# Attention step of a retention + mixture-of-experts kernel: the next step's scores moved behind the values, and the values' matmuls grouped by row half

## The chip, the cores and the metric

The program runs on one core of one Trainium2 chip. The time is the device time of one execution in microseconds. The kernel before takes 430.98 us (median of three timed runs, 430.73 to 432.25).

## The reference

Queries, keys and values are float32 of shape batch 8, heads 8, sequence 576, head dimension 64. Each head has a decay gamma; there is no softmax, so the attention is a masked and decayed product:

```python
scores = scale * np.matmul(q, k.transpose(0, 1, 3, 2))
Dmat = np.where(rel >= 0, gamma[:, None, None] ** rel[None, :, :], 0.0)
ret = scores * Dmat[None, :, :, :]
attn_out = np.matmul(ret, v)
```

The result, seen as 4608 tokens of 512 numbers (`x`), goes through one routed expert layer. A token with `x @ w_skip <= 0` is passed on unchanged. Each other token goes to the expert with the largest `x @ w_gate` (8 experts, hidden width 1024), and its output is `x + gate * (relu(x @ w1[e]) @ w2[e])`.

## The kernel before

**Two phases.** The first (some 157 us) is the attention and, beside it, the routing of the tokens; the second runs the experts. The change is in the first.

**Tiles of the attention.** The 4608 tokens are 36 tiles of 128 rows (`NT`), numbered `g`. Two batches are 9 tiles (`NPD`), so `place(g) = g % 9` is a tile's place; at place 0 a sequence begins, and at place 4 one ends in the first 64 rows and the next begins. The decays are powers of gamma, so a causal product over the whole sequence is taken as a product inside the tile plus a running 64x64 state per head:

- `load_u(g)` loads the tile: queries and keys by head (first half of `u`), values and keys by row (second half). Five tiles fit (`UBUFS`); tile `g + 4` is loaded into the buffer that tile `g - 1` leaves.
- `scale(g)` (L478): GpSimd multiplies the values by gamma to the minus position, in `u` itself.
- `scores(g)` (L446): eight matmuls, contraction 64, 128 columns, on the upper and lower half of the array's rows in turn (`r` = 0, 1). Half `r` fills the PSUM tile `psc[r]`, one bank each.
- `causal(g)` (L461): VectorE multiplies the two PSUM tiles by the mask and writes `sc` to SBUF, first `r` = 0, then `r` = 1.
- `state(g)` (L483): eight matmuls of 128 rows, 64 columns, which add the tile's keys times values to `ps_s`; ScalarE copies that to `st` for the next tile. None at place 8.
- `values(g)` (L503): eight matmuls (128 rows, 64 columns) of the scores with the values (L513), then eight with the state of the tiles before (64 rows, 64 columns, L527; none at place 0), all added up in two PSUM tiles `pxt` (names `xt0`, `xt1`). VectorE multiplies these by the decays into `xt` (L540).
- `stage_c(g)` (L547): four transposes, a copy by ScalarE and the store of the tile to `out`.

**Order.** TensorE's instructions stand in the order in which the code is written (a manual schedule for this engine). The other engines' orders are set by a scheduler, which places the routing's many small VectorE operations between `causal` and `xt`; each engine then runs its list strictly in order. One iteration `g` of the loop (L663 to L687) writes: `load_u(g + 4)`, `scale(g + 1)`, `scores(g + 1)`, `causal(g + 1)`, some filler matmuls in the first two iterations (`keep_up`), `state(g)`, `values(g)`, `stage_c(g - 1)`, and then routing matmuls. So the scores of a tile are made one iteration ahead of its values.

**Routing.** Every fourth iteration `logits_a` (L556) multiplies four tiles of `xt` by the gate weights, and an iteration later `logits_b` (L571) transposes the result (`pn`). After each group of 8, 8, 8, 4, 4, 4 tiles, `route_a` and `route_b` pick the expert, count, and rank the tokens in some 35 VectorE operations of 8 to 64 numbers a partition (L148 to L205), and `slot_match` (L212) makes one one-hot matrix a tile, which TensorE multiplies (L217). Near the end `close_first` (L266) gives the row numbers `gi` (L279) for the first gather of tokens from `out` (L287, GpSimd), behind which GpSimd splits the first experts' weights (L613).

Of the kernel before, what the change touches and what calls it, by code (L numbers as in the profile page):

```python
# [26 lines left out]
NPR = H // 2  # L27
# [30 lines left out]
def kernel(  # L58
# [25 lines left out]
    def keep_up(n):  # L84
        for _ in range(n):
            nc.tensor.matmul(ps_m, warm[:, :P], warm, start=True, stop=True)
# [312 lines left out]
    with ExitStack() as actx:  # L399
# [13 lines left out]
        def load_u(g):  # L413
            u_t[g] = ap.tile([P, 4, DM], F32, tag="u", name=f"u_{g}", bufs=UBUFS)
            for s in range(2):
                nc.sync.dma_start(u_t[g][:, 2 * s : 2 * s + 2].rearrange("p s i -> p (s i)"), qkv[g, s])
# [23 lines left out]
        def head(a, r):  # L440
            return 2 * a + (r ^ (a & 1))

        def place(g):
            return g % NPD

        def scores(g):  # L446

            u = u_t[g].rearrange("p s (a i) -> p s a i", a=NPR)
            psc_t[g] = [pp.tile([P, NPR, P], F32, tag=f"sc{r}", name=f"psc{r}_{g}") for r in range(2)]
            for a in range(NPR):  # L450
                for r in range(2):
                    nc.tensor.matmul(  # L452
                        psc_t[g][r][:, a, :],
                        u[halves[r], 1, a, :],
                        u[halves[r], 0, a, :],
                        start=a == 0,
                        stop=a == NPR - 1,
                        skip_group_check=True,
                    )

        def causal(g):  # L461

            sc_t[g] = ap.tile([P, 2, NPR, P], F32, tag="sc", name=f"sc_{g}")
            m = masks[place(g) == NPD // 2].unsqueeze(1).broadcast_to([P, NPR, P])
            for r, ps in enumerate(psc_t.pop(g)):
                nc.vector.tensor_tensor(sc_t[g][:, r], ps, m, ALU.mult)  # L466

        def decays(g):
            c0 = 2 * g % NQ
            ins = nc.vector.tensor_tensor(  # L470
                gt_sb[:, c0 : c0 + 2],
                gt_sb[:, 0:2],
                qt_sb[:, c0 : c0 + 2, :].unsqueeze(3).broadcast_to([P, 2, NPR, D]),
                ALU.mult,
            )
            tc.keep_in_program_order(ins)

        def scale(g):  # L478

            v = u_t[g][:, 2].rearrange("p (h i) -> p h i", h=H)  # L480
            nc.gpsimd.tensor_tensor(v, v, vt_sb[:, place(g), :].unsqueeze(2).broadcast_to([P, H, D]), ALU.mult)  # L481

        def state(g):  # L483

            t = place(g)
            if t == NPD - 1:
                return
            rows = slice(D, P) if t == NPD // 2 else slice(0, P)
            v, k = (u_t[g][rows, 2 + s].rearrange("p (h i) -> p h i", h=H) for s in range(2))
            for a in range(NPR):  # L490
                for r in range(2):
                    nc.tensor.matmul(
                        ps_s[halves[r], a, :],
                        k[:, head(a, r), :],
                        v[:, head(a, r), :],
                        start=t in (0, NPD // 2) and a == 0,
                        stop=a == NPR - 1,
                        skip_group_check=True,
                    )
            st_t[g + 1] = ap.tile([P, NPR, D], F32, tag="st", name=f"st_{g + 1}")  # L500
            nc.scalar.copy(st_t[g + 1], ps_s)

        def values(g):  # L503

            u = u_t[g].rearrange("p s (a i) -> p s a i", a=NPR)
            v = u_t[g][:, 2].rearrange("p (h i) -> p h i", h=H)
            pxt = px_t[g] = [pp.tile([P, NPR // 2, P], F32, tag=f"xt{e}", name=f"pxt{e}_{g}") for e in range(2)]
            sc = sc_t.pop(g)
            t = place(g)
            for a in range(NPR):  # L510
                for r in range(2):
                    j = head(a, r) % 2
                    nc.tensor.matmul(  # L513
                        pxt[a % 2][halves[j], a // 2, :],
                        v[:, head(a, r), :],
                        sc[:, r, a, :],
                        start=a < 2,
                        stop=t == 0 and a >= NPR - 2,
                        skip_group_check=True,
                    )  # L520
            if t:
                n = D if t == NPD // 2 else P
                st = st_t.pop(g)
                for a in range(NPR):
                    for r in range(2):
                        j = head(a, r) % 2
                        nc.tensor.matmul(  # L527
                            pxt[a % 2][halves[j], a // 2, :n],
                            st[halves[r], a, :],
                            u[halves[r], 0, a, :n],  # L530
                            start=False,
                            stop=a >= NPR - 2,
                            skip_group_check=True,
                        )
            b, o = divmod(g, NB)
            if o == 0:
                xt_t[b] = ap.tile([P, NPR, NB * P], F32, tag="xt", name=f"xt_{b}")
            c0 = 2 * g % NQ
            for e in range(2):
                nc.vector.tensor_tensor(  # L540
                    xt_t[b][:, e::2, o * P : (o + 1) * P].rearrange("p a (c i) -> p a c i", c=2),
                    pxt[e].rearrange("p a (c i) -> p a c i", c=2),
                    gt_sb[:, c0 : c0 + 2, e::2].rearrange("p c a i -> p a c i"),
                    ALU.mult,
                )

        def stage_c(g):  # L547
            b, o = divmod(g, NB)
            px = pp.tile([P, DM], F32, tag="xn", name=f"px_{g}")
            for c in range(NCC):  # L550
                nc.tensor.transpose(px[:, c * P : (c + 1) * P], xt_t[b][:, c, o * P : (o + 1) * P], ident)  # L551
            xn = ap.tile([P, DM], F32, tag="xn", name=f"xn_{g}")
            nc.scalar.copy(xn, px)  # L553
            nc.scalar.dma_start(out[g * P : (g + 1) * P, :], xn)
# [16 lines left out]
        def logits_b(b, lt):  # L571
            pn = pp.tile([P, NB, P], F32, tag="lg", name=f"pn_{b}")
            for o in range(NB):
                nc.tensor.transpose(pn[:, o, :], lt[:, o * P : (o + 1) * P], ident)
            nc.vector.tensor_reduce(
                lg[:, b * NB : (b + 1) * NB, :],
                pn.rearrange("p t (c w) -> p t w c", w=WP)[:, :, :NW, :],
                axis=AX.X,
                op=ALU.add,
            )  # L580
# [45 lines left out]
        def routing(most):  # L626

            for do in added:
                do()
            added.clear()  # L630
            for n in range(most):
                if not todo or len(added) == NR or todo[0][1] > g or (n and todo[0][0]):
                    break
                todo.pop(0)[2]()
# [28 lines left out]
        for g in range(NT):  # L663
            ahead = g + 1 < NT
            if g + UAHEAD < NT:
                load_u(g + UAHEAD)
            if ahead:
                scale(g + 1)
                scores(g + 1)
                causal(g + 1)  # L670
            if g < len(NKEEP):
                keep_up(NKEEP[g])
            state(g)
            values(g)
            if g < 4:
                decays(g + 1)
            if g:
                stage_c(g - 1)
            if lt is None:
                routing(1 if g == NT - 1 else 3 if g < starts[KCUT + 1] else 8)  # L680
            if lt is not None:
                logits_b(g // NB - 1 - (g % NB < 2), lt)
                route(g // NB - 1 - (g % NB < 2))
                lt = None
            if g > NB and g % NB == 1:
                lt = logits_a(g // NB - 1)
            weights()  # L687
        g = NT
# [328 lines left out]
```

## Time and profile before

| | us |
|---|---|
| median of the timed runs | 430.98 |
| the profiled execution's own time | 431.52 |
| its span, first to last instruction | 429.8 |
| attention phase, first scores to the last values' transposes | 5.7 to 157.3 |
| TensorE busy over the span | 408.5 (95%) |
| VectorE busy over the span | 270.5 (63%) |
| granted TensorE clock, mean | 0.982 |

The span is 1.7 us shorter than the time of the same execution; what lies around it is launch and end. TensorE's busy time is a union of modelled matmul times, so it says that work was in flight, and not that the array ran at its peak. A float32 matmul of the program shows as two records, so eight matmuls are "x16"; only a transpose is one record. Weight loads are shown as an engine of their own (PEld).

### The profile page before, as it was taken

The page shows a single profiled execution, that of the slowest core. Times are in us where ns is not written, and L with a number is a line of the kernel's source. Part 1 is how long each engine was busy: PE and PEld are TensorE (multiplying, and loading weights), DVE is VectorE, ACT ScalarE, POOL GpSimd, SP SyncE. Part 2 cuts the span into 40 slices and gives each one's busy share as a digit, 9 for nine tenths or more (in the row PEclk, how much of TensorE's full clock was granted, in tenths as well). Part 3 has the DMA queues.
Part 4 walks back from the last instruction along what each step waited for, and adds up shares of the span by engine and source line. Part 5 has one row for each costly group of instructions (what it writes and reads, how often), then busy time and mean ns, then how long its engine had stood idle before and what let it go on. Part 6 is the DMA issues. An engine that isn't in the chain of part 4 may idle for free. (4 is left out here: it accounts for less than half of the span.)

```text
span 429.8 us, 10717 instructions
## 1 busy us (share of the span) xinstructions
PE 408.5 (95%) x4303; PEld 363.1 (84%) x4303; DVE 270.5 (63%) x636; ACT 152.6 (36%) x264; POOL 115.1 (27%) x133
## 2 busy tenths in 40 slices
PE   7999999999999968999999999999999999999990
PEld 3878778777787855888999999999999999999990
DVE  3665596596488989738655654875655655656421
ACT  1222322222223443117434434434444445445210
POOL 4332232122123475150330042032141230400402
PEclk9999999999999996999999999999999999999995
DMA  8999998998899764355663445455465465642101
GB/s 316 397 363 322 356 317 282 316 318 278 304 325 355 310 192 152 101 149 202 202 227 128 146 168 197 148 165 194 148 203 165 158 203 188 208 132 95 51 2 52
DMA packets 28869, 91.71 MB, mean 213 GB/s; under 512 B 4104, under 2 KB 4232, under 8 KB 28817
## 3 DMA queue, kind: packets, MB, share of 16 engines
q1 hardware_dynamic: 19584, 71.31, 49.2%
q0 software_dynamic: 3616, 9.86, 6.8%
q10 hardware_dynamic: 5616, 9.82, 6.0%
q8 instruction: 35, 0.57, 0.5%
q14 instruction: 18, 0.14, 0.1%
HBM read 76.80 MB, written 14.55 MB: 213 GB/s over the span
## 5 line engine op out<-in xcount | busy, mean ns | idle before, releaser
L137 DVE TENSOR_TENSOR wlo_w<-w,whi_w 128x1024 fp32r<-128x1024 f32 x59 | 71.9, 1223 | 62.3 <-ACT whi_w L136 62.3
L136 ACT CAST whi_w<-w 128x1024 fp32r<-128x1024 f32 x59 | 61.7, 1051 | 61.3 <-PE py L371 59.8
L800 POOL DMA_INDIRECT out<-rs,sidx x24 | 32.8, 1367 | 158.3 <-DVE rs L799 155.0
L371 PE MATMUL py<-hhi,whi_w 128*128 128x344 f32 (+6 forms) x224 | 70.7, 316 | 0.0
L371 PE MATMUL ph<-xhi,whi_w 128*128 128x344 f32 (+6 forms) x224 | 68.9, 307 | 0.0
L371 PE MATMUL ph<-xhi,wlo_w 128*128 128x344 f32 (+6 forms) x224 | 67.8, 302 | 0.0
L371 PE MATMUL ph<-xlo,whi_w 128*128 128x344 f32 (+6 forms) x224 | 67.7, 302 | 0.0
L371 PE MATMUL py<-hlo,whi_w 128*128 128x344 f32 (+6 forms) x224 | 67.6, 302 | 0.0
L371 PE MATMUL py<-hhi,wlo_w 128*128 128x344 f32 (+6 forms) x224 | 67.6, 302 | 0.0
L481 POOL TENSOR_TENSOR u<-u,tt_sb 128x512 f32<-128x512 f32 x36 | 38.3, 1063 | 104.6 <-DMA u<-qkv 88.3
L466 DVE TENSOR_TENSOR sc<-psc,mask 128x512 f32<-128x512 f32 x72 | 46.6, 684 | 25.6 <-PE psc L452 25.6
L379 ACT ACTIVATE hhi<-ph 128x344 fp32r<-128x344 f32 (+8 forms) x61 | 26.0, 427 | 64.6 <-PE ph L371 59.0
L452 PEld LDWEIGHTS psc<-u 64*128 64x128 f32 x576 | 36.7, 187 | 13.6 <-DVE xt L540 5.4
L452 PE MATMUL psc<-u 64*128 64x128 f32 x576 | 44.3, 285 | 2.2 <-DMA u<-qkv 1.3
L553 ACT COPY xn<-px 128x512 f32<-128x512 f32 x36 | 21.1, 586 | 64.4 <-PE px L551 44.1
L371 PEld LDWEIGHTS py<-hhi,whi_w 128*128 128x128 f32 x224 | 42.2, 188 | 0.9
L371 PEld LDWEIGHTS ph<-xhi,whi_w 128*128 128x128 f32 x224 | 42.2, 188 | 0.2
L371 PEld LDWEIGHTS ph<-xlo,whi_w 128*128 128x128 f32 x224 | 42.2, 188 | 0.1
L371 PEld LDWEIGHTS py<-hlo,whi_w 128*128 128x128 f32 x224 | 42.2, 189 | 0.0
L371 PEld LDWEIGHTS ph<-xhi,wlo_w 128*128 128x128 f32 x224 | 42.2, 189 | 0.0
L371 PEld LDWEIGHTS py<-hhi,wlo_w 128*128 128x128 f32 x224 | 42.2, 188 | 0.0
L380 DVE SCALAR_TENSOR_TENSOR hlo<-ph,hhi 128x344 fp32r<-128x344 f32 (+8 forms) x61 | 28.9, 474 | 15.8 <-ACT hhi L379 14.8
(179 smaller groups left out, 616.6 us busy)
## 6 DMA issues: line engine op xcount, KB each, us to landing
u<-qkv SPq DMA_DIRECT2D x72, 512.0 KB, 6.6
w<-w SPq DMA_DIRECT2D x64, 512.0 KB, 3.6
out<-xn ACTq DMA_DIRECT2D x36, 256.0 KB, 6.7
out<-rs,sidx POOLq DMA_INDIRECT x24, 4.8
xg<-out,gidx POOLq DMA_INDIRECT x21, 5.1
gt_sb<-gtab ACTq DMA_DIRECT2D x1, 256.0 KB, 5.7
wg_sb<-wg ACTq DMA_DIRECT2D x1, 64.0 KB, 6.7
tt_sb<-ttab ACTq DMA_DIRECT2D x1, 56.0 KB
```

What stands on the lines that cost most here:

```text
L136: nc.scalar.copy(hi, t)
L137: nc.vector.tensor_tensor(lo, t, hi.bitcast(F32), ALU.subtract)
L371: nc.tensor.matmul(ps, x, y, start=first and n == 0, stop=last and n == 3 * len(terms) - 1)
L379: nc.scalar.activation(hi, ph, AF.Relu)
L380: nc.vector.scalar_tensor_tensor(lo, ph, 0.0, hi.bitcast(F32), ALU.max, ALU.subtract)
L452: nc.tensor.matmul(psc_t[g][r][:, a, :], u[halves[r], 1, a, :], u[halves[r], 0, a, :], start=a == 0, stop=a == NPR - 1, skip_group_check=True,
L466: nc.vector.tensor_tensor(sc_t[g][:, r], ps, m, ALU.mult)
L481: nc.gpsimd.tensor_tensor(v, v, vt_sb[:, place(g), :].unsqueeze(2).broadcast_to([P, H, D]), ALU.mult)
L553: nc.scalar.copy(xn, px)
L800: put = nc.gpsimd.indirect_dma_start(out=out, out_offset=bass.IndirectOffsetOnAxis(ap=sidx[:n, k, e : e + 1], axis=0), in_=rs[:n], in_offs ...
```

## The change

Two edits. In `values`, the loop over the row half `r` is now outside the loop over the pairs `a`: the four matmuls that read `sc[:, 0]` come first, then the four that read `sc[:, 1]`. In the iteration, `state(g)` and `values(g)` now come before `scores(g + 1)` and `causal(g + 1)`.

```diff
@@ -507,8 +507,8 @@
             pxt = px_t[g] = [pp.tile([P, NPR // 2, P], F32, tag=f"xt{e}", name=f"pxt{e}_{g}") for e in range(2)]
             sc = sc_t.pop(g)
             t = place(g)
-            for a in range(NPR):
-                for r in range(2):
+            for r in range(2):
+                for a in range(NPR):
                     j = head(a, r) % 2
                     nc.tensor.matmul(
                         pxt[a % 2][halves[j], a // 2, :],
@@ -666,12 +666,13 @@
                 load_u(g + UAHEAD)
             if ahead:
                 scale(g + 1)
+            state(g)
+            values(g)
+            if ahead:
                 scores(g + 1)
                 causal(g + 1)
             if g < len(NKEEP):
                 keep_up(NKEEP[g])
-            state(g)
-            values(g)
             if g < 4:
                 decays(g + 1)
             if g:
```

TensorE in iteration 11, before (the names are those of the text above; a number behind a name is the buffer's, the bracket names the semaphores waited for, by the engine that raises them; rows that read like the one above them but for the buffer are left out):

```order
L452 MATMUL psc_12_823<-u_634 128x128 [waits DMAHW1_49,DVE_49]
L452 MATMUL psc_12_824<-u_634 128x128 [waits DVE_49]
L492 MATMUL ps_s<-u_579 64x64 [waits DMAHW0_49,Activation_49,Pool_49]
L492 MATMUL ps_s<-u_579 64x64 x7
L513 MATMUL pxt_11_846<-sc_748,u_579 64x128 [waits DVE_49]
L513 MATMUL pxt_11_847<-sc_748,u_579 64x128 [waits DVE_49]
L527 MATMUL pxt_11_846<-u_579,st_759 64x128 x2
L551 MATMUL px_866<-ident,xt_669 128x128 [waits Activation_49]
```

The same iteration of the change:

```order
L492 MATMUL ps_s<-u_579 64x64 [waits DMAHW7_49,Activation_49,Pool_49]
L492 MATMUL ps_s<-u_579 64x64 x7
L513 MATMUL pxt_11_833<-sc_778,u_579 64x128 [waits DVE_49]
L513 MATMUL pxt_11_834<-sc_778,u_579 64x128 [waits PE_49]
L513 MATMUL pxt_11_833<-sc_778,u_579 64x128 [waits DVE_49]
L527 MATMUL pxt_11_833<-u_579,st_746 64x128 x2
L452 MATMUL psc_12_853<-u_634 128x128 [waits DMAHW1_49,PE_49]
L551 MATMUL px_866<-ident,xt_656 128x128 [waits Activation_49]
```

The scores of tile 12 have moved from ahead of the state to behind the state's part of the values (L527), next to the transposes. The second `DVE_49` wait of L513 stands at the fifth matmul of the eight, the first of row half 1.

VectorE between the mask products of tiles 11 and 12, before (first group of eight tiles being routed; of the routing's rows only the ends of each run are shown):

```order
L540 TENSOR_TENSOR xt_669<-pxt_10_762,gt_sb 128x2x128
L575 TENSOR_REDUCE lg<-pn_789 128x36
L161 SCALAR_TENSOR_TENSOR mk_806<-lg,oh_801 128x64
L466 TENSOR_TENSOR sc_833<-psc_12_823,mask_160 128x512
L466 TENSOR_TENSOR sc_833<-psc_12_824,mask_160 128x512
L191 TENSOR_TENSOR gt_935<-gt_935,cp_937 128x8
L540 TENSOR_TENSOR xt_669<-pxt_11_846,gt_sb 128x2x128
L540 TENSOR_TENSOR xt_669<-pxt_11_847,gt_sb 128x2x128
L193 TENSOR_TENSOR mc<-mks,cp_937 128x320
L466 TENSOR_TENSOR sc_888<-psc_13_878,mask_163 128x512
```

The same stretch of the change:

```order
L466 TENSOR_TENSOR sc_778<-psc_11_769,mask_160 128x512
L575 TENSOR_REDUCE lg<-pn_789 128x36
L161 SCALAR_TENSOR_TENSOR mk_806<-lg,oh_801 128x64
L188 CAST cp_937<-gt_935 128x8
L540 TENSOR_TENSOR xt_656<-pxt_11_833,gt_sb 128x2x128
L540 TENSOR_TENSOR xt_656<-pxt_11_834,gt_sb 128x2x128
L193 TENSOR_TENSOR mc<-mks,cp_937 128x320
L169 CAST cb_817<-cum 128x72
L466 TENSOR_TENSOR sc_863<-psc_12_853,mask_160 128x512
L466 TENSOR_TENSOR sc_863<-psc_12_854,mask_160 128x512
```

Before, nine routing operations stand ahead of the first half of tile 12's mask product, two between its halves, and eleven behind it. In the change all of them stand ahead of it: 14 ahead of `xt` of tile 11, one between its halves, and 11 behind. The group of tiles 12 to 19 is placed alike (same counts) between the mask products of tiles 19 and 20; the third group stands as 5, 1, 10, 1 and 11 operations around tiles 27 and 28, and the first group of four as 13, 1 and 7 around tiles 31 and 32. No instruction is added or taken away on any engine, and SyncE's list of loads is the same.

## The prediction

> **What bounds the kernel now.** I read the windows first, for who is busy in the phase that the change touches, and where that ends (columns: length, then busy time and count of TensorE, its weight loads, VectorE, ScalarE, GpSimd; then granted clock, DMA share, GB/s).
>
> ```profile
> 20.00:40.00 20.00, 20.00 (x352) 16.09 (x351) 11.52 (x24) 5.38 (x11) 6.28 (x6) 1.00 0.97 352
> 157.00:163.10 6.10, 0.72 (x5) 0.47 (x6) 5.96 (x14) 2.65 (x4) 6.10 (x10) 0.89 0.77 236
> 200.00:430.00 230.00, 218.98 (x1543) 212.36 (x1541) 128.25 (x204) 95.63 (x151) 50.05 (x39) 0.98 0.47 155
> ```
>
> In the attention TensorE never pauses and VectorE is little over half busy; behind its end VectorE is full and TensorE waits; the experts are TensorE's again. DMA is at 0.97, so the waits come next: TensorE waited for a load once in the phase, for 1.3 us.
>
> ```profile
> PE psc L452 <- DMA u<-qkv: 1.3, 1, 1.3
> ```
>
> Then the timeline of TensorE over one iteration (start, length, line, tile of the array, count):
>
> ```profile
> 35.53 0.66 PE L551 MATMUL px<-ident,xt 128*128 128x128 f32 x4
> 36.02 0.60 PE L574 MATMUL pn<-ident,lt 128*128 128x128 f32 x4
> 36.55 1.16 PE L452 MATMUL psc<-u 64*128 64x128 f32 x16
> 37.64 0.69 PE L492 MATMUL ps_s<-u 128*64 128x64 f32 x16
> 38.16 1.05 PE L513 MATMUL pxt<-sc,u 128*64 128x128 f32 x16
> 39.14 0.67 PE L527 MATMUL pxt<-u,st 64*64 64x128 f32 x16
> 39.73 0.66 PE L551 MATMUL px<-ident,xt 128*128 128x128 f32 x4
> 40.32 1.16 PE L452 MATMUL psc<-u 64*128 64x128 f32 x16
> ```
>
> From start to start: scores 1.09, state 0.52, values 0.98, state's part 0.59, transposes 0.59: a plain iteration is 3.77 us of TensorE's own issue, back to back. An iteration with `logits_b` has 0.49 for the transposes and 0.53 for `pn`, 4.20 in all. So the attention is bound by TensorE's instruction stream, and its pauses are few. They stand where the routing loads VectorE (a scores group is 1.16 long when nothing holds it; the bracket is idle time and who ended it):
>
> ```profile
> 55.76 1.47 PE L452 MATMUL psc<-u 64*128 64x128 f32 x16
> 59.84 0.19 PE L176 MATMUL ps_m<-cb,ones 128*128 128x64 bf16 x1
> 60.35 1.75 PE L452 MATMUL psc<-u 64*128 64x128 f32 x16 [0.32 <-DVE sc L466]
> 89.63 1.56 PE L452 MATMUL psc<-u 64*128 64x128 f32 x16
> 91.12 0.69 PE L492 MATMUL ps_s<-u 128*64 128x64 f32 x16
> 92.23 1.28 PE L513 MATMUL pxt<-sc,u 128*64 128x128 f32 x16 [0.42 <-DVE xt L540]
> 95.10 1.75 PE L452 MATMUL psc<-u 64*128 64x128 f32 x16 [0.34 <-DVE sc L466]
> 124.38 1.38 PE L452 MATMUL psc<-u 64*128 64x128 f32 x16
> 128.30 0.19 PE L176 MATMUL ps_m<-cb,ones 128*128 128x64 bf16 x1
> 128.42 1.64 PE L452 MATMUL psc<-u 64*128 64x128 f32 x16
> ```
>
> First group of eight: 0.31, then 0.59 inside and 0.39 ahead (0.51 behind L176, against 0.12 at 128.30): 1.3. Second: 0.40, 0.59 (1.11 behind the state, against 0.52), 0.23, 0.59 and, taken as in the first, 0.4: 2.2. Third: 0.22 and 0.48: 0.7. In all 4.2 us, all from late mask products or `xt`.
>
> **What the change does to a plain iteration.** It adds no instruction. SyncE's loads keep their order; on ScalarE the copy of the state now stands ahead of a tile's store instead of behind it, and nothing waits for that store soon. TensorE's stream becomes state, values, state's part, scores, transposes. Its sum stays 3.77, since each of the four changes of tile shape stays, with other neighbours (the second rival doubts this). What is new is a short loop. Before, a mask product was made a whole iteration ahead of the values that read it. Now the scores, the mask product and the values follow each other, and only transposes (0.59) and state (0.52) lie between. How fast VectorE answers:
>
> ```profile
> 69.99 1.16 PE L452 MATMUL psc<-u 64*128 64x128 f32 x16
> 71.18 1.29 DVE L466 TENSOR_TENSOR sc<-psc,mask 128x512 f32<-128x512 f32 x2 [0.78 <-PE psc L452]
> 72.57 0.67 PE L527 MATMUL pxt<-u,st 64*64 64x128 f32 x16
> 73.27 0.42 DVE L540 TENSOR_TENSOR xt<-pxt,gt_sb 128x256 f32<-128x256 f32 x1 [0.81 <-PE pxt L527]
> ```
>
> The mask product starts 1.19 behind the first of the scores, its first half is done 0.68 later and the second at 1.19 + 1.29 = 2.48. With 0.05 for the semaphore (estimated from the 0.03 between the end of the scores at 71.15 and 71.18), row half 0 may start at 1.92 and row half 1 at 2.53. TensorE gets to the values at 1.09 + 0.59 + 0.52 = 2.20, and to row half 1 half of 0.98 later, some 2.64. So both just fit, with 0.28 and 0.11 to spare, and the regrouping by row half is what makes the second fit. A plain iteration costs nothing while VectorE is free at the moment the scores end. That is its price: VectorE's `xt` starts 0.70 behind the state's part, which is 1.68 behind the values; with 0.74 for the pair VectorE is free 0.33 ahead of the next mask product, and between a mask product's end and the next `xt` there are 1.4 us. Routing work beyond these two gaps now stops TensorE. In tile place 8 there is no state to cover: values at 1.68 against 1.92 is 0.24, and row half 1 another 0.15; tiles 8 and 17 pay some 0.35 each (tiles 26 and 35 have logits work ahead): **0.7**.
>
> **The four bursts.** VectorE's rows of the first one:
>
> ```profile
> 52.10 0.31 DVE L575 TENSOR_REDUCE lg<-pn 128x36 f32<-128x144 f32 x1 [0.27 <-PE pn L574]
> 54.48 0.83 DVE L165 TENSOR_TENSOR cum<-cum,mk 128x8 f32<-128x8 f32 x1
> 55.94 0.15 DVE L165 TENSOR_TENSOR cum<-cum,mk 128x8 f32<-128x8 f32 x1
> 58.08 1.34 DVE L193 TENSOR_TENSOR mc<-mks,cp 128x320 bf16<-128x320 bf16 x1
> 127.16 0.49 DVE L193 TENSOR_TENSOR mc<-mks,cp 128x320 bf16<-128x320 bf16 x1
> 59.61 1.28 DVE L466 TENSOR_TENSOR sc<-psc,mask 128x512 f32<-128x512 f32 x2
> 60.81 0.74 DVE L540 TENSOR_TENSOR xt<-pxt,gt_sb 128x256 f32<-128x256 f32 x2
> ```
>
> From 52.10 to the end of L193 at 59.42 VectorE does, without a pause, 26 routing operations, one mask product and one pair of `xt`. The new order has just these between the start of tile 11's mask product and that of tile 12's. So the second starts 7.3 us behind the first, where TensorE's iteration is 4.20: 3.1 late. Two of the operations met a GpSimd instruction (0.83 against 0.15; 1.34 against 0.49), some 1.5 us; without them it is 1.6 late. From this goes the 0.28 to spare, and 0.16 comes on top because row half 1 then follows by 0.60 instead of 0.44: the pause is 1.5 to 3.0. GpSimd's `scale` falls about once into each iteration, so one meeting is likelier than none or two: **2.3**. The second burst has the same order: **2.3**. By 0.15 us an operation ((7.3 - 1.5 - 1.9) / 26), the third (5 ahead of `xt`, which fit; then 11, or 1.7, in a gap of 0.33, some of them cheaper ones) gives 0.7 to 1.5, I take **1.1**; the fourth (13, or 2.0, in a gap of 1.8, then 8, or 1.2, in 0.33) 0.4 to 1.3, **0.8**. The runs of five one-hot matrices (L212) mostly fit the 1.4: 0 to 0.9 in all, **0.2**. Gross 2.3 + 2.3 + 1.1 + 0.8 + 0.7 + 0.2 = 7.4.
>
> **What comes off.** The 4.2 of pauses above have the same bursts as cause and are replaced, not kept. The start gains something:
>
> ```profile
> 6.69 1.04 POOL L481 TENSOR_TENSOR u<-u,tt_sb 128x512 f32<-128x512 f32 x1 [3.12 <-DMA u<-qkv]
> 8.18 1.26 PE L452 MATMUL psc<-u 64*128 64x128 f32 x16 [1.35 <-DMA u<-qkv]
> ```
>
> Tile 0's state now fills the wait for tile 1's load, but not ahead of its `scale`, done at 7.73: 8.18 - 7.73 = 0.45. At the end VectorE and GpSimd set the pace (second window row), so the question is when the last routing there starts.
>
> ```profile
> 155.78 0.31 DVE L575 TENSOR_REDUCE lg<-pn 128x36 f32<-128x144 f32 x1 [0.35 <-PE pn L574]
> 156.89 0.66 PE L551 MATMUL px<-ident,xt 128*128 128x128 f32 x4
> ```
>
> Before, 1.11 ahead of TensorE's last transposes. Now it follows tile 35's mask product, 2.48 behind its scores, while TensorE still does 1.09 + 0.49 + 0.53 + 0.98 + 0.59 = 3.68 from there: 1.2 ahead. So that chain moves with TensorE, less 0.1, and what follows (the experts, TensorE busy 219 of 230 us in the third window row) moves along. Sum: 7.4 - 4.2 - 0.45 - 0.1 = +2.65 on the profiled execution's 431.5 (span 429.8 and 1.7 around it), thus 434.2; that execution was 0.5 over the median, so **433.6** for the median. With the low ends (1.5, 1.5, 0.7, 0.4, 0.6, 0: 4.7) it is -0.05 or 430.9, with the high ones (3.0, 3.0, 1.5, 1.3, 0.8, 0.9: 10.5) +5.7 or 436.7.
>
> **Rivals.** *The bursts cost no more than before.* The routing work is the same and TensorE already paused for it; then only 0.45 and 0.1 are left: 430.4. For it speaks that the scheduler could spread the work; against it, that it did not (the order of the first burst), and that the lead of a whole iteration is gone.
>
> *Fewer changes of array shape.* State's part and scores now stand together, both on half the rows. If only the row half counted, one change fewer an iteration would be paid: transposes take 0.49 to start `pn` in the same shape and 0.59 to start scores, and the first matmul behind a change shows 0.1 more:
>
> ```profile
> L452 PE MATMUL psc<-u x576: 272/272/373, 5.7 to 151.9; 64*128 64x128 f32 x192
> 23.88 1.16 PE L452 MATMUL psc<-u 64*128 64x128 f32 x16
> 24.97 0.68 PE L492 MATMUL ps_s<-u 64*64 64x64 f32 x16
> ```
>
> 0.2 in 32 iterations is 6.4 us: 427.4, or 430.6 if only the 0.1 of the gap goes. Against it: tile 4's state uses half the rows (64*64) behind scores of 64*128, just the reverse pair, and starts 1.09 behind them, no sooner than a 128*64 state does. The Trainium skill says the same as a rule (TensorEngine Tiling (Array Packing), Key Properties): a change of tiling mode, not of tile, drains the engine, and 64x64 and 64x128 are two modes; by that rule nothing comes off the sum, and the row of tile 4 agrees.
>
> *Every iteration waits.* The 0.28 and 0.11 are small. If the answer of VectorE comes 0.3 later than I have it, row half 1 misses by 0.2 in the some 20 iterations without logits work or burst: 4 us, 437.8. It decides from 0.11 on. For it: the thin margin, which rests on one semaphore delay; against it: both ends of it are rows.
>
> **Chances.** Bursts as summed 58%; absorbed 18%; shape changes 10%; every iteration 14%. A measurement of this kernel tells about 0.5% from no change, 428.8 to 433.1. Of the first case two thirds lie above 433.1 and the rest within; absorbed is within but for 2%; shape changes is faster in four of five; the last is slower. Faster 10%, same 38%, slower 52%. The range goes from 429.0, which leaves out most of the shape case, to 437.5.
>
> **What would show it.** In the new profile the waits should list TensorE's values (L513) behind the mask product (L466) as the longest, with 2 us or more each near 57 and 94 us and under 0.5 in tiles 8 and 17, and nothing in plain iterations, which stay at 3.77. Scores should never wait. A step at 3.57 would show the shape rival, one near 4.0 the last. I am wrong if the values' waits come to less than 5 us or more than 10.5 in all, or if VectorE reaches the routing earlier than its order makes me think.

## The result, and the profile after

The changed kernel took 436.45 us (median of five executions, 434.98 to 438.12); the kernel before took 430.88 us beside it. The ratio is 1.0142, with a 95% interval from 1.0115 to 1.0168: slower by 1.4%. Measured twice more, beside other experiments, it was 1.0175 (1.0131 to 1.0219) and 1.0103 (1.0066 to 1.0139). Forecast were +2.65 us and 433.6; it came to +5.6. The direction and the place were right and the time lies inside the stated range (429.0 to 437.5), but the loss that was forecast is less than half of the measured one.

The profiled execution of the change is the longest of the five: 438.12 us, span 436.4, against 431.52 and 429.8 before. So in this pair of profiles 6.6 us have to be found. The list of waits for the attention (8 to 163 us; engine, tile and line, what it waited for, then total, count and longest):

```profile
PEld pxt L513 <- DVE sc L466: 7.0, 9, 2.7
PE pxt L513 <- DVE sc L466: 5.3, 3, 2.6
```

The values now wait for the mask product, and that is TensorE's longest wait of the stage; scores wait no longer. The timeline of TensorE shows where (start, length, line, then idle time and its releaser in brackets):

```profile
17.78 1.16 PE L452 MATMUL psc<-u 64*128 64x128 f32 x16
18.87 0.65 PE L551 MATMUL px<-ident,xt 128*128 128x128 f32 x4
19.46 0.69 PE L492 MATMUL ps_s<-u 128*64 128x64 f32 x16
19.97 1.04 PE L513 MATMUL pxt<-sc,u 128*64 128x128 f32 x16
20.95 0.67 PE L527 MATMUL pxt<-u,st 64*64 64x128 f32 x16
21.54 0.71 PE L452 MATMUL psc<-u 64*128 64x128 f32 x8
...
39.08 0.66 PE L551 MATMUL px<-ident,xt 128*128 128x128 f32 x4
39.97 1.21 PE L513 MATMUL pxt<-sc,u 128*64 128x128 f32 x16 [0.24 <-issue]
...
55.52 0.69 PE L492 MATMUL ps_s<-u 128*64 128x64 f32 x16
58.76 1.72 PE L513 MATMUL pxt<-sc,u 128*64 128x128 f32 x16 [2.56 <-DVE sc L466]
60.41 1.13 PE L527 MATMUL pxt<-u,st 64*64 64x128 f32 x16
61.48 1.73 PE L452 MATMUL psc<-u 64*128 64x128 f32 x16
63.13 0.66 PE L551 MATMUL px<-ident,xt 128*128 128x128 f32 x4
...
92.67 0.69 PE L492 MATMUL ps_s<-u 128*64 128x64 f32 x16
95.15 1.26 PE L513 MATMUL pxt<-sc,u 128*64 128x128 f32 x16 [1.80 <-DVE sc L466]
96.33 0.71 PE L527 MATMUL pxt<-u,st 64*64 64x128 f32 x16
96.97 2.08 PE L452 MATMUL psc<-u 64*128 64x128 f32 x16
98.98 1.12 PE L551 MATMUL px<-ident,xt 128*128 128x128 f32 x4
...
130.47 1.33 PE L513 MATMUL pxt<-sc,u 128*64 128x128 f32 x16 [0.93 <-DVE sc L466]
...
148.26 1.25 PE L513 MATMUL pxt<-sc,u 128*64 128x128 f32 x16
...
162.94 0.66 PE L551 MATMUL px<-ident,xt 128*128 128x128 f32 x4
169.78 0.19 PE L176 MATMUL ps_m<-cb,ones 128*128 128x32 bf16 x1 [3.24 <-DVE cb L169]
```

A plain iteration (17.78 to 21.54) is still 3.76, with no wait in it. In the first burst the values start 3.24 behind the state instead of 0.52. What was not foreseen stands in the rows behind: state's part takes 1.13 where 17.18 to 20.95 had 0.67, scores take 1.73 and, in the second burst, 2.08 where 1.16 is normal. No wait is listed there; the matmuls themselves are slow. The windows say why (length, busy time and count of TensorE, its loads, VectorE, ScalarE, GpSimd, then granted clock):

```profile
55.87:59.28 3.41, 0.85 (x20) 0.61 (x16) 3.41 (x14) 0.71 (x2) 1.12 (x1) 1.00 0.98 332
59.28:62.70 3.42, 3.42 (x38) 2.68 (x36) 0.94 (x5) 0.00 (x0) 1.04 (x1) 0.50 0.36 120
93.42:96.83 3.41, 1.68 (x32) 1.26 (x32) 2.42 (x12) 0.35 (x1) 1.04 (x1) 1.00 0.86 302
96.83:100.25 3.42, 3.42 (x32) 2.90 (x26) 1.92 (x4) 0.11 (x1) 1.04 (x1) 0.50 0.75 226
```

Behind each of the two long pauses TensorE ran at half its clock for 3.41 us. The kernel before has no such stretch inside its attention.

The ledger of this execution, against the forecast's terms. An excess is a group's length, or its distance to the group ahead, less the usual one (values 1.05, state to values 0.52, state's part 0.67, scores 1.16):

| term | forecast | measured |
|---|---|---|
| first burst, waits (tile 12) | 2.3 | 2.73 + 0.21 = 2.9 |
| second burst, waits (tile 20) | 2.3 | 1.97 + 0.21 = 2.2 |
| third burst (tiles 28, 29) | 1.1 | 1.38 + 0.51 = 1.9 |
| fourth burst (tile 32) | 0.8 | 0.3 |
| tiles 8, 17 and 35, runs of one-hot matrices | 0.9 | 0.46 + 0.16 + 0.11 = 0.7 |
| half clock | none | 1.5 + 1.5 = 3.0 |
| pauses of before that come off | -4.2 | -4.2 |
| start | -0.45 | -0.6 |
| sum at the attention's last transposes | 2.75 | 6.2 (read: 162.94 - 156.89 = 6.05) |
| end, behind these transposes | -0.1 | +0.5 |

The waits alone are 8.0 against 7.4. The half clock is the term that was missing.

### The profile page after: what moved, and what is told of

It is laid out like the page before. It is cut to its first block, busy times and chain, and to the rows that moved or that the text cites. A ratio compares the mean times of both kernels' runs of the same rounds, so it can differ in the third digit from the quotient of the medians.

```text
span 436.4 us, 10712 instructions
## 1 busy us (share of the span) xinstructions
PE 410.1 (94%) x4301; PEld 364.3 (83%) x4303; DVE 269.3 (62%) x636; ACT 152.5 (35%) x264; POOL 114.7 (26%) x133
## 5 line engine op out<-in xcount | busy, mean ns | idle before, releaser
L540 DVE TENSOR_TENSOR xt<-pxt,gt_sb 128x256 f32<-128x256 f32 x72 | 27.5, 418 | 36.4 <-PE pxt L527 32.4
L513 PE MATMUL pxt<-sc,u 128*64 128x128 f32 x576 | 39.9, 278 | 5.7 <-DVE sc L466 5.3
L452 PE MATMUL psc<-u 64*128 64x128 f32 x576 | 43.3, 291 | 0.0
```

Source lines behind the costliest of these rows:

```text
L452: nc.tensor.matmul(psc_t[g][r][:, a, :], u[halves[r], 1, a, :], u[halves[r], 0, a, :], start=a == 0, stop=a == NPR - 1, skip_group_check=True,
L513: nc.tensor.matmul(pxt[a % 2][halves[j], a // 2, :], v[:, head(a, r), :], sc[:, r, a, :], start=a < 2, stop=t == 0 and a >= NPR - 2, skip_ ...
L540: nc.vector.tensor_tensor(xt_t[b][:, e::2, o * P : (o + 1) * P].rearrange("p a (c i) -> p a c i", c=2), pxt[e].rearrange("p a (c i) -> p a ...
```

## The experiments

**Both parts apart.** First the row-half loop alone, in the old order of an iteration.

```diff
-            for a in range(NPR):
-                for r in range(2):
+            for r in range(2):
+                for a in range(NPR):
```

> The old order of an iteration, and of the change only the loop by row half. My theory: the values read a mask product that is an iteration old, so neither half waits; a plain iteration stays 3.77 us and the time stays at before, 430.9 within 0.5%. Rival (the new order of the 16 matmuls costs by itself, through the array's tiles or PSUM): values longer than 1.05 us in every tile, 0.1 x 36 or more, 434.5 and up.

It ran at 1.0009 of before (0.9982 to 1.0036), and iterations in its trace are 3.77. So the loop by itself costs nothing that this interval shows. The pauses that TensorE has in this trace (0.52 at tile 12, 1.60 around tile 20, 0.21 at 103 us, 0.79 at tile 28) come to 3.1, where the profile of before had 4.2 in the same order of an iteration. These are two kernels with one profile each; since the loop adds no wait, I take the 1 us for a difference between executions.

Then the new order of an iteration with the old loop in the values.

```diff
-            for r in range(2):
-                for a in range(NPR):
+            for a in range(NPR):
+                for r in range(2):
```

> The new order of an iteration with the old loop in the values (by pair, then row half). My theory: the second matmul already needs row half 1, which is ready 2.53 us behind the start of the scores while TensorE is there at 2.26, so plain iterations wait 0.27 inside the values and take 4.04; in some 20 of them 5.4 us, so 441 to 443 against the change's 436.45. Rival (the row-half order is of no use): plain iterations at 3.77, 435 to 438.

It took 440.18 us, 1.0255 of before (1.0212 to 1.0299), where the change has 1.0142. TensorE's timeline, a plain iteration and one with logits work:

```profile
28.35 1.43 PE L513 MATMUL pxt<-sc,u 128*64 128x128 f32 x16
29.71 0.67 PE L527 MATMUL pxt<-u,st 64*64 64x128 f32 x16
...
33.50 1.05 PE L513 MATMUL pxt<-sc,u 128*64 128x128 f32 x16
```

In tiles 3, 5 and 9, where only transposes and state stand between scores and values, the values take 0.38 longer (1.43 against 1.05): I had 0.27. With logits work there, nothing is lost, and fewer iterations wait than the 20 that I reckoned. So row half 1 comes some 0.11 later than reckoned, which uses up the 0.11 that the forecast had to spare; still no plain iteration of the change waits, and the row-half loop is what saves them.

**Where the loss is made.** The old order put back around the bursts.

```diff
+            old = 9 <= g <= 13 or 17 <= g <= 21 or 25 <= g <= 33
+            if ahead and old:
+                scores(g + 1)
+                causal(g + 1)
             state(g)
             values(g)
-            if ahead:
+            if ahead and not old:
```

> The new order only in tiles 0-8, 14-16, 22-24 and 34-35; the old order in tiles 9-13, 17-21 and 25-33, where the routing loads VectorE. The values by row half in all. Theory A (the loss is made where routing falls between scores and values): the pauses of 2 to 3 us near 57 and 95 us are gone, the old ones (some 4.2 us in all) are back, no half clock, time 430.4 to 431.5. Rival B (the shorter loop costs in every iteration a little): at least a third of the loss stays, 432.7 and up.

The ratio is 1.0048 (1.0028 to 1.0068): two thirds of the loss gone, not all. The third that stays is where the range of rival B begins, so the ratio alone does not decide between the two; the trace does. The long pauses of the values are gone and no stretch of half clock is left in the attention. But each switch from the new order to the old sets two groups of scores behind each other with only transposes between, and the second must wait until the mask product has read the first:

```profile
43.22 0.66 PE L551 MATMUL px<-ident,xt 128*128 128x128 f32 x4
44.06 1.75 PE L452 MATMUL psc<-u 64*128 64x128 f32 x16 [0.19 <-DVE sc L466]
```

That is 0.26 ahead and 0.59 inside; with 0.63 at each of the other two switches (78.7 and 113.4 us) 2.1 us, all of the 1.0048. I had left the switch out. By this reading the loss sits at the bursts, and what is left is the price of the switches.

**The routing dealt out.** In the new order, VectorE's routing for the first two groups of eight is cut into pieces, one to an iteration, each pinned behind a mask product (the gates and the product `mc` likewise; the one-hot matrices of these groups are pinned too). TensorE's matmuls of these groups (L175, L176) come an iteration later with it.

```diff
-        for t in range(n):
-            nc.vector.tensor_tensor(cum[:, t0 + t + 1, :], ...)
+        def count(pin):
+            for t in range(n):
+                add = nc.vector.tensor_tensor(cum[:, t0 + t + 1, :], ...)
+                if pin and t == 0:
+                    tc.keep_in_program_order(add)
+        if t0 + n <= starts[KONE]:
+            counts.append(count)
...
                 causal(g + 1)
+            if counts:
+                counts.pop(0)(True)
```

> The changed kernel with VectorE's routing work for the first two groups of eight dealt out: mask of the choice in one iteration, running sums in the next, gates in the next, the product and the one-hot matrices behind that, each piece pinned behind a mask product. Theory A (the pauses of tiles 12 and 20 come from VectorE's order alone): these two pauses (2.9 and 2.2 us) and the half clock behind them are gone, the later two bursts stay; against before 0.995 to 0.999, 428.5 to 430.5 where before is 430.9. Rival B (VectorE has too little room in the short loop, however its work is dealt out): the pause is found again in pieces of 0.3 to 1 us behind it, and the ratio stays over 1.005.

> The same dealing out in the kernel before (old order of an iteration, old loop in the values). Theory A: its pauses in the first two groups (1.3 and 2.2 us) go, ratio 0.991 to 0.994. If so the change is still behind by its other terms, 0.4% or more. Rival B (an iteration of lead already hides what can be hidden): 0.998 to 1.002.

> The changed kernel once more, beside the next two on one chip. The ratio to before should be 1.014 again, with runs spread over some 3 us. Theory A (a pause near 57 or 94 us is followed by 3.41 us at half clock in some runs): the profiled run has none, one or both of these stretches, and its span lies 1.5 us higher for each. Rival B: the span does not go with the stretches.

These three ran on one chip. The change alone: 1.0175. Dealt out: 1.0039 (1.0017 to 1.0061), so by the medians (437.21, 431.87 and, before, 430.18) 5.3 us of 7.0 are back. The waits of its attention:

```profile
PEld pxt L534 <- DVE sc L487: 3.7, 12, 1.2
PE pxt L534 <- DVE sc L487: 1.5, 3, 1.1
```

1.5 us is left of the 4.4 to 5.3 that the three profiles of the change have in the second row; the longest, 1.1, is the third burst, which was not touched. The values of tiles 12 and 20 start without a wait; 0.45 turns up at tile 13, and 0.2 and 0.6 at tiles 20 and 21. There is no half clock in the attention. So VectorE's order makes the two long pauses, as theory A has it. The pieces that stay behind are what rival B foretold, and the ratio is half a per cent over the forecast of theory A; how much of that the pieces make is not worked out.

The same in the kernel before gave 1.0006 (0.9986 to 1.0026), not 0.991 to 0.994: the number of rival B. In its trace tile 12 has no pause, but 1.3 us stay around tile 20, so there was little to be had: with an iteration of lead the burst cost less to begin with (3.1 to 4.2 in all).

For three groups instead of two:

> The dealt-out routing of VectorE for the first three groups of eight instead of two, in the new order. Theory A (the third burst, 1.5 to 2.1 us, has the same cause): that pause shrinks under 0.7 us, and the ratio to before falls from 1.004 to 0.999 to 1.002; later work is pushed on by some iterations, so the pause of the fourth burst (tile 32) may grow by up to 1 us, which would leave 1.002 to 1.004. Rival B (the third burst does not come from the order of VectorE): ratio and pause stay.

1.0159 (1.0120 to 1.0198): neither theory's range. The third burst shrank to 0.8, but tile 32 grew to 1.55, as feared, and behind the attention this came:

```profile
141.96 1.25 PE L534 MATMUL pxt<-sc,u 128*64 128x128 f32 x16 [1.17 <-DVE sc L487]
...
163.61 0.47 PE L608 MATMUL pt_early<-ident,xg 128*128 128x128 f32 x1 [5.89 <-DMA xg<-out,gi]
...
174.21 0.75 PE L238 MATMUL ps_m<-mc,r 128*128 128x40 bf16 x12 [2.76 <-DVE mc L210]
```

VectorE makes the indices of the first expert's gather at 159.4 us, behind the attention, where the kernel with two groups dealt out has them at 152.0; TensorE waits 5.9 us for the rows. VectorE stands idle for 7.0 us up to 166.54, until the same rows have passed TensorE and ScalarE; the last group's routing comes behind that in its list, and TensorE waits 2.8 us more for `mc`. The kernel with two groups waits there too (1.6 and 3.9 us, for VectorE), so the waits are not the price. The price is the difference: the values of tile 35 start 0.5 us later with three groups (155.29 against 154.80), so nothing was won in the attention as a whole, and from there to the end it takes 6.2 us longer. No version here beat the kernel before.

**The half clock: rule and price.** In the second profile of the change (435.77 us, span 434.1 against 436.4) one of the two long pauses is followed by half clock, the other is not, though both are 1.8 us of idle time. The span is 2.3 shorter: 1.5 for the stretch and 0.8 for the shorter first pause, while 0.8 more in the later bursts and 0.8 less behind the attention cancel.

```profile
55.98:59.40 3.42, 1.67 (x34) 1.18 (x34) 2.88 (x13) 0.54 (x2) 1.04 (x1) 1.00 0.95 340
59.40:62.81 3.41, 3.41 (x35) 2.79 (x26) 1.58 (x4) 0.00 (x0) 0.80 (x1) 0.50 0.66 207
90.12:93.53 3.41, 2.41 (x42) 1.94 (x36) 3.41 (x20) 0.96 (x2) 0.86 (x1) 1.00 0.92 317
93.53:96.94 3.41, 2.62 (x46) 2.09 (x48) 2.37 (x8) 0.00 (x0) 1.04 (x1) 1.00 0.77 300
96.94:100.36 3.42, 3.42 (x66) 2.89 (x66) 3.02 (x11) 0.96 (x2) 1.04 (x1) 1.00 0.91 277
```

The clock changes lie on a grid: in the first profile half clock begins at 59.28, 96.83 and 168.51, that is 11 and 21 steps of 3.413 us apart. Where the pause falls into one step (busy 1.67 of 3.42) the next step is slow; where the grid cuts it in two (2.41 and 2.62) it is not. To test this, pauses were made in quiet iterations: the second half of some mask products is taken again in place, with a mask of zeros and ones, so no value changes.

```diff
+            for _ in range(DOSE.get(g, 0)):
+                nc.vector.tensor_tensor(sc_t[g][:, 1], sc_t[g][:, 1], m, ALU.mult)
```

> The changed kernel with the second half of the mask product of tiles 5, 7, 9, 15, 17, 23 and 25 taken 3, 4, 3, 5, 4, 3 and 2 times more (the mask is 0 or 1, so nothing changes in value): pauses of TensorE of some 1.1 to 2.9 us in quiet iterations. Theory A (the clock is set anew every 3.41 us by TensorE's busy share of the stretch before; in the first traces 0.49 was followed by half clock, 0.56 was not): every stretch with a share under 0.5, and no other, is followed by one at half clock, whatever the length of the pause. Rival B (the length of the pause decides): every pause over 1.7 us is followed by half clock. Rival C (a whole idle stretch is needed): no half clock before 160 us but that of the routing bursts.

> The same extra mask products as in the kernel with pauses before, with other counts: tiles 5, 7, 9, 15, 17, 23 and 25 taken 4, 3, 2, 4, 3, 5 and 3 times more. Theory A (busy share of the 3.41 us stretch): at full clock, every stretch in which TensorE is busy for less than 0.49 is followed by one at half clock, and none with more than 0.52. Rival B (length of the pause): some stretch breaks this line while the pauses sort the cases, those over 1.7 us with half clock and those under it without.

The pauses came out at 1.0 to 3.7 us of idle time, some longer than reckoned, and the kernels (one execution each) at 461.6 and 455.4 us. Of the first, two cases near the line:

```profile
27.41:30.82 3.41, 1.50 (x31) 1.10 (x30) 3.04 (x5) 0.96 (x2) 1.30 (x2) 1.00 0.98 351
30.82:34.24 3.42, 3.42 (x40) 2.76 (x36) 0.75 (x2) 0.00 (x0) 1.62 (x2) 0.50 0.56 204
...
112.74:116.16 3.42, 1.84 (x32) 1.42 (x29) 3.42 (x15) 0.96 (x2) 1.04 (x1) 1.00 0.89 253
116.16:119.57 3.41, 3.23 (x51) 2.59 (x52) 1.89 (x7) 0.00 (x0) 0.61 (x1) 1.00 0.59 192
```

Of the second, a pause of 2.28 us of idle time that the grid cuts:

```profile
89.50:92.92 3.42, 1.89 (x29) 1.44 (x27) 3.00 (x5) 0.59 (x1) 1.04 (x1) 1.00 0.93 296
92.92:96.33 3.41, 2.64 (x43) 2.18 (x44) 1.72 (x4) 0.00 (x0) 1.04 (x1) 1.00 0.42 143
96.33:99.74 3.41, 3.41 (x55) 2.23 (x55) 1.62 (x4) 1.55 (x3) 0.00 (x0) 1.00 0.90 265
```

That pause left the clock at full. One of the same 2.28 us in the first of the two kernels (at 43.62), one of 1.91 (that of the first row above) and one of 1.75 in the change were followed by half clock. So length does not sort them (rival B falls), and no step has to be idle throughout (rival C falls); the busy share sorts them. I cut all 14 traces of this study, both profiles of the prediction's pair among them, on their own grids: of the steps at full clock up to the last matmul, all 29 with a share (of modelled matmul time) up to 0.49 are followed by half clock, and none of the 1639 with 0.51 or more. The Trainium skill (TensorE: Matmul & The Clock Gate, Part 1: The HAM clock gate) has the window of 3.4 us that runs freely, which the grid confirms, but lets the clock fall behind an idle window; here half an idle window was enough (a share of 0.49).

The price, measured by iteration (first of the values to first of the next values): tile 12 to 13 takes 5.63, 5.68 and 5.68 in the three profiles of the change, all with half clock there, and 4.13 in both profiles of the next kernel, which has none; tile 20 to 21 takes 5.54 with and 4.03 without. So 1.5 us for a stretch.

That next kernel keeps TensorE busy during the two pauses.

```diff
             state(g)
+            if g in FILL:                      # {12: 13, 20: 9}
+                px = pp.tile([P, NB, P], F32, tag="lg", name=f"fill_{g}")
+                for n in range(FILL[g]):
+                    nc.tensor.transpose(px[:, n % NB, :], ident, ident)
             values(g)
```

> The changed kernel with 13 and 9 idle transposes (never read) put ahead of the values of tiles 12 and 20, some 1.9 and 1.3 us of TensorE work inside the two long pauses. Theory A (the pauses themselves cost some 4.7 us, and the half clock that follows them in some runs costs 1.5 us each): the values start no earlier than in the change, but no stretch of clock 0.5 stands between 20 and 160 us; runs lie within 1 us of each other, at 434.5 to 435.3. Rival B (the pauses are the whole loss, the clock record is without effect): 436.4, spread over 435 to 438 as the change is.

> The changed kernel beside the filled one, so that the price of the half clock is measured on one chip. Theory A (half clock behind some of the long pauses): 1.014 to 1.018 of before, runs spread over 3 us or more. Rival B (waits alone): the same time as the filled kernel beside it, within 0.2%.

> The changed kernel with the idle transposes inside the pauses of tiles 12 and 20, on the same chip as the changed kernel alone. Theory A: the values start as late as without them, no half clock between 20 and 155 us, and the ratio to before is 1.007 to 1.011, 0.4 to 0.8% under the changed kernel beside it. Rival B: no difference to it, 1.014 to 1.018.

In both profiles the clock stays at 1.00 throughout the attention. Where the fill decides that can be read on the grid, at tile 20 of the first profile and at tile 12 of the second:

```profile
91.55:94.96 3.41, 1.93 (x24) 1.51 (x23) 3.13 (x10) 0.24 (x1) 1.12 (x1) 1.00 0.80 291
94.96:98.37 3.41, 3.41 (x68) 2.88 (x66) 2.17 (x5) 0.59 (x1) 1.04 (x1) 1.00 0.53 162
...
56.40:59.81 3.41, 2.63 (x29) 2.09 (x28) 2.98 (x9) 0.35 (x1) 0.88 (x1) 1.00 0.79 278
59.81:63.22 3.41, 3.41 (x66) 2.94 (x64) 2.29 (x6) 0.59 (x1) 0.71 (x1) 1.00 0.53 165
```

With the fill these two steps have shares of 0.57 and 0.77; with the time of its transposes taken off they would have 0.29 and 0.33, and half clock would follow by the rule. The other two pauses prove nothing, since the grid cuts them: even without the fill no share there falls under 0.51.

The times do not agree with each other. First the filled kernel took 433.59 us, 1.0093 (1.0061 to 1.0124). As a distance to before that is what theory A expects, though its executions spread over 2.0 us and not 1. On another chip, beside the change, it took 437.05, 1.0138 (1.0105 to 1.0171), and the change 435.15, 1.0103: theory A's order reversed. In that pair of profiles (435.92 and 435.34) the filled kernel is 1.55 shorter behind tile 12, and longer by 0.62 at tile 12, 0.80 at tile 32 and 0.38 at tile 35. The first two go with VectorE operations that met GpSimd (next section); that explains the profiled pair, not the whole difference of the medians, which stays open. So the half clock and its 1.5 us in an iteration are shown; that filling the pauses pays is not.

What the half clock does to whole executions can be read from the change's 17 timed ones, by the mean clock that each was granted (one stretch lowers it by 0.5 x 3.41 / 436 = 0.004): six at 0.983 to 0.985 took 434.1 to 435.0, median 434.8; six at 0.981 to 0.982 median 436.5; five at 0.975 to 0.977 took 437.0 to 438.9, median 437.5. That is the spread of the change, and 2.7 us between none and two. This goes together; other stretches, at the end of the attention, also move the mean.

## Why the prediction was wrong in size

*Plain iterations at 3.77, margins of 0.28 and 0.11.* Right: there is no wait in them, though the second margin is hardly there, and taking the row-half loop away costs 0.38 in tiles 3, 5 and 9. With that *every iteration waits* falls. *Fewer changes of array shape* falls by the row at 20.95: state's part to scores is 0.59, as before any other shape; the rule cited there agrees. (From 433.6 the rivals' sums come to 427.2, 430.4 and 437.6, each 0.2 under the time given; nothing rests on that.)

*Tile place 8, 0.7.* Right: tile 8 pays 0.30 (39.08 to 39.97 is 0.89 against 0.59) and 0.16; tile 17 only 0.16, since one-hot matmuls stood ahead of it, and tile 35 0.11 (0.6 in the third profile).

*The first two bursts, 2.3 each, 1.5 to 3.0.* Right, with the reason. VectorE's rows of the first one:

```profile
50.83 1.29 DVE L466 TENSOR_TENSOR sc<-psc,mask 128x512 f32<-128x512 f32 x2 [0.33 <-PE psc L452]
...
53.91 0.94 DVE L165 TENSOR_TENSOR cum<-cum,mk 128x8 f32<-128x8 f32 x1
...
57.07 1.04 DVE L169 CAST cb<-cum 128x72 bf16<-128x72 f32 x1
58.03 1.27 DVE L466 TENSOR_TENSOR sc<-psc,mask 128x512 f32<-128x512 f32 x2
...
161.79 0.31 DVE L575 TENSOR_REDUCE lg<-pn 128x36 f32<-128x144 f32 x1
```

Two of 26 routing operations took 0.94 and 1.04 instead of some 0.15: they met GpSimd's products, which ran from 53.79 to 54.83 and from 56.94 to 58.06. The mask product starts 7.20 behind the last one (58.03 - 50.83); with one such meeting it was 6.38 and 6.37 in the other two profiles, and the wait 2.1. *Absorbed* falls: the waits are longer, not the same.

*Third 1.1, fourth 0.8.* The third was 1.9, 2.1 and 1.9 in the three profiles, above its range; it met GpSimd twice each time, which I had not counted there. The fourth was 0.3, 0.9 and 0.3: 0.9 where an operation took 0.79, 0.3 where none did. Together they came to 2.2, 3.0 and 2.2 against 1.9. Gross, the waits came to 8.0, 8.0 and 7.6 against 7.4.

*What comes off, 4.2.* Taken from one execution; the old order with the row-half loop has 3.1 in its profile. *Start, 0.45:* 0.6. *End, -0.1:* routing starts 1.15 ahead of the last transposes, as before (1.11), so the step was right; but from there to L176 it took 8.0 us against 7.3, with L181 (0.76, beside GpSimd) now ahead of L169. L181 stands there in all three profiles of the change (8.0, 7.8 and 7.6 us), yet behind the last transposes the second and third run 0.3 and 0.5 us shorter than before, and only the first 0.5 longer. So I count the longer end as chance.

**The step that failed** is the sum "7.4 - 4.2 - 0.45 - 0.1": it prices a pause of TensorE at its own length. A pause that leaves TensorE under half busy in one step of 3.41 us costs another 1.5 us. With 3.0 or 1.5 for that, and 3.1 to 4.2 coming off, the same sum gives +4.2 to +6.8, and the three measurements are +4.3, +5.6 and +7.0, the last just outside. That 436.45 lies inside the stated range is luck: the range reached so far up for waits of 10.5 us, and the waits were 8.0; the half clock, priced at nothing, filled the rest. The profile of before held the sign: its windows show 0.89 of clock at 157 to 163 us, which I quoted and read as an idle engine. And the correction to the median (0.5 under the profile) missed the other way: the profiled execution of the change lies 1.7 over its median.

## What to carry to other kernels

A reordering that shortens the way from a producer to its reader is priced in the iterations where the producer's engine has other work, not in the plain ones: list what that engine does between the two, and subtract the cover that is left. Where a pause takes more than half of a clock step on TensorE, price it with the slow matmuls behind it, and expect the executions to spread, since the grid of the steps decides which pauses count. Work that is moved out of the way must be followed to its last reader: dealing out a third group shortened that group's pause, made the next one longer, and delayed a gather and what stood behind it, 6.2 us in all behind the attention.

## What the runs showed of the hardware that was not expected

The clock falls by busy share, not by idle time: up to 0.49 of 3.41 us always, from 0.51 never, in 1668 steps of full clock. At half clock, 18 steps with a share up to 0.866 were followed by half clock again, and 29 with 0.868 or more by full clock. The grid does not start with the kernel: full clock first came 4.1 to 7.0 us into an execution, and the first scores started between 5.3 and 6.5 us accordingly.

Small VectorE operations can be held up by a GpSimd instruction that runs at the same time. Of the operations that take up to 0.26 us as a rule, 85 took more than 0.4 us in the first 165 us of the 14 traces, up to 1.10, and all 85 met a GpSimd product (1.04 us in the attention). Not every meeting costs: no reduction and no reciprocal is among the 85. One such meeting more or less in a burst moves its pause by up to 0.8 us from one execution to the next, which is as much as this kernel's other terms.
